# Order rules for VectorE's score tiles in a kernel with an order planned at build time

## The chip, the cores and the metric

One core of one Trainium2 chip. The metric is the device time of one execution in microseconds, the median of several runs. An execution has five engines with a queue of instructions each: TensorE (matmuls), VectorE, ScalarE, GpSimd and SyncE (which issues most DMAs).

## The reference

Two independent parts of 2048 tokens and width 640 are computed and laid side by side in the output of 1280 columns.

```python
# part A: a diagonal state-space layer, a recurrence over the tokens
Bu = einsum("bld,pd->blp", x, B_bar)
h = Lam_bar * h + Bu[:, t]                        # complex, for each t
y = 2 * einsum("blp,dp->bld", hs, C).real + x * Dskip
# part B: attention with 32 heads of width 20 that share one key and one value
q = (x @ wq).reshape(B, S, 32, 20); k = x @ wk; v = x @ wv
p = softmax(q @ k.T * 20 ** -0.5)
out = (p @ v).reshape(B, S, 640) @ wo
```

## The kernel before

**Tiles.** The scores of part B are cut into 2048 tiles of 128 keys x 512 queries of one head. A *block* is a group of four heads for 512 queries: 64 tiles, 16 of each head; there are 32 blocks. Part A, the projections and the output products run as tasks beside them.

**Two ways to the exponential.** A tile's scores are made by one matmul of 32 rows (`score`). Then either ScalarE computes exp of two or three tiles at once from PSUM into a ring `PR` of 24 columns (L1378), or VectorE reads the tile from PSUM into an integer buffer of `BIG` (`fill_d`, L1569; the page shows it as L811), an approximate exponential in the bits of a bf16. VectorE's way needs four versions of the tile (`SHIFTS`): the first read and three copies with a number added, made by VectorE (L811, BIG<-BIG) or GpSimd (L1673). Each version takes a buffer of its own until it has been used; `d_free` lists the free ones. A tile of ScalarE costs one matmul with V (PV, MB<-PR,VP), a tile of VectorE four (MB<-BIG,VS). PV matmuls of the four heads of a block run as a quad, side by side in four column groups.

**PSUM.** There are two *slots* of three banks each (SC) and two single banks (MB): one for the sums of PV, one for tasks. A fill (`fill`) writes a slot with three score matmuls. If the third bank is given to VectorE (`own`), ScalarE's exp covers two tiles; otherwise it covers three. A slot can be filled again when both its exp and VectorE's read of its third bank are done. VectorE may also get tiles in a free task bank (`extra`, `d_source`).

**The order.** Every instruction is a step with an assumed duration; at build time a list scheduler (`Schedule`) plays the engines forward, takes at each moment the ready step of the best priority, and so writes down one fixed order for each engine. Twelve such orders are made, eleven of them with small random shifts of the tasks' due times, and the one with the earliest planned end is built. Waits are semaphores placed from that order. So a rule changed in the choice of tiles changes the order of all engines from there on.

**Choice of VectorE's tiles.** `want_own` and `want_d` limit their share (`SHARE` 0.29 of all tiles so far) and ask for free buffers. `take_d` takes the tile from the block that `d_block` names: the current one, `act_block`, while more than `AHEAD` = 10 of its tiles remain, else the next. Of the block's four heads it takes the one with the fewest tiles given to VectorE (`d_turn`). `can_d` refuses a tile of a block that PV has not come to yet (`b > self.pv_b`) unless as many buffers are free as a tile needs plus all copies still due for the block in hand (`due_copies`).

**What waits for what.** An exp waits for its fill and for its columns of `PR` to have been read by PV (`h.prev` in `fill`). PV of a block starts after that of the block before has been read out (L1740).

Of the kernel before, what the change touches and what calls it, by code (L numbers as in the profile page):

```python
# [43 lines left out]
class Schedule:  # L44
# [13 lines left out]
    EARLIER = {"dve": 40.0, "act": 8.0}  # L58
# [371 lines left out]
class Build:  # L430
# [477 lines left out]
    def constants(self):  # L908
# [14 lines left out]
        def select(t, pattern, op, v, base, mult, dur):  # L923
            return "pool", lambda e: e.affine_select(out=t, in_=t, pattern=pattern, compare_op=op, fill=v, base=base,
                                                     channel_multiplier=mult), dur
        adds = next(x for x in library_config.all_libraries if bass_isa.InstInt64Add in x.instructions)
        self.adds_op = self.pool(lambda e: e.load_library(adds), 100, prio=0.1)
        many("ident", [fill(p.ident[:], 0.0, 110),
                       select(p.ident[:], [[-1, 128]], ALU.not_equal, 1.0, 0, 1, 300)])
        one = bass.AP(tensor=p.one, offset=0, ap=[[1, 128], [0, 256]])  # L930
        many("iota", [fill(p.one[:], 1.0, 80),
                      ("dve", lambda e: e.tensor_tensor_scan(p.iota[:], one, one, -1.0, ALU.mult, ALU.add), 670)])
        self.c_op["wkz"] = self.dve(lambda e: e.memset(p.wkr[:], 0.0), 110, writes=["wkr"], prio=0.2)
        many("tload", [fill(p.tload[:], 0.0, 80)])
        many("VP", [fill(p.VP[:], 0.0, 280), fill(p.VP[:, :, 20:21], 1.0, 100)])
        many("VZ", [fill(p.VZ[:], 0.0, 80)])
# [405 lines left out]
    def fill(self, op, i):  # L1342
        p = self
        t, banks = self.slots[i]
        n = min(self.cap[i], NTILE - self.tile_n)
        extra, used, own = [], set(), None
        if n == 3 and self.want_own():
            own = self.take_d(used)
        if own is not None:
            n = 2  # L1350
        while len(extra) < 4 - self.cap[i] and self.want_d(len(extra), own is not None):
            m = self.take_d(used)
            if m is None:
                break
            extra.append(m)
        tiles = [self.take_tile(used) for _ in range(n)]
        h = self.pr_take(n)
        keys = [f"PR{h.index + x}" for x in range(n)]
        ents = []
        for x, m in enumerate(tiles):  # L1360
            b, kc, j = self.score(op, m, t[:, 512 * x:512 * x + 512], banks[x])
            ents.append((b, kc, j, p.PR[:, h.index + x, :]))
        first = [] if own is None else [self.fill_d(op, own, banks[2])]
        if first:
            other = self.slot_last[1 - i][0]
            begin = self.s.t + self.mmt(512, 4) + 200
            if other.eng == "act":
                begin = max(begin, other.start + other.dur if other.start is not None else self.s.t + other.dur)
            first[0].due = begin + 2 * (0.8333 * 1024 + 64) - self.REFILL
        for m in extra:  # L1370
            self.fill_d(op, m)
        n_mm = len(op.fns)
        self.board(op, used)
        op.reads = sorted(set(op.reads))
        op.dur = self.mmt(512, n_mm + (len(op.fns) > n_mm))
        op.load = 128.0 * n_mm
        dst = p.PR[:, h.index:h.index + n, :]
        ex = self.act(lambda e: e.activation(dst, t[:, 0:512 * n], ACT.Exp, scale=1.0 / UNIT),  # L1378
                      0.8333 * 512 * n + 64, table="exp",
                      deps=[op], reads=[b.key for b in banks[:n]], writes=keys, prio=0.5,  # L1380
                      gate=lambda: all(x.taken and x.left == 0 and self.s.done(x.users) for x in h.prev))

        def on_start(_):
            h.taken, h.left, h.prev = True, n, []
            self.waiting.remove(h)
        self.waiting.append(h)
        ex.hook = on_start
        self.slot_last[i] = [ex] + first
        for (b, kc, j, rhs), key in zip(ents, keys):
            self.pvq[b][j].append((p.VP[:, kc, 0:32], kc, rhs, key, ex, h, "VP"))  # L1390
            self.pv_filled[b] += 1
# [35 lines left out]
    def want_own(self):  # L1427
# [4 lines left out]
        self.firsts = [o for o in self.firsts if o.start is None]  # L1432
        return len(self.d_free()) > len(self.SHIFTS) - 1

    firsts = []
    LAG = 120

# [42 lines left out]
        self.tile_n += 1  # L1480
        return 64 * b + 4 * self.rem[b][j].popleft() + j

    AHEAD = 10

    def d_block(self):

        b = self.act_block()
        return b if self.remaining(b) > self.AHEAD else b + 1

    def take_d(self, used):  # L1490

# [9 lines left out]
    def can_d(self):  # L1501
        b = self.d_block()
        if b >= NQB * NGG or not self.block_ready(b):
            return False
        if not self.block_seen(b):
            return False
        if b > self.pv_b and len(self.d_free()) < len(self.SHIFTS) + self.due_copies():
            return False
        return bool(self.rem[b][self.d_turn(b)])

# [948 lines left out]
```

## Time and profile before

| | us |
|---|---|
| median of 3 runs | 716.0 (715.95 to 716.43) |
| span of the profiled execution, first to last instruction | 714.5 |
| ScalarE busy | 695.0 |
| TensorE busy | 694.9 |
| VectorE busy | 627.5 |
| GpSimd busy | 429.3 |
| first exp starts | 21.17 |
| last exp ends | 704.76 |

The page gives no time of the profiled execution beside its span; the runs' times lie some 1.5 us above it. The granted TensorE clock is 1.000 over the span. TensorE's busy time is modelled at its ends: a matmul of 512 columns shows 0.38 us, while such matmuls follow each other some 0.22 us apart. In the rows below PEld are TensorE's weight loads, which carry its waits; "MB<-PR,VP" names what is written and what is read. A program's line L674 or L811 is a helper's, so the tiles tell the steps apart.

### The profile page before, as it was taken

The page shows a single profiled execution, that of the slowest core. Times are in us where ns is not written, and L with a number is a line of the kernel's source. Part 1 is how long each engine was busy: PE and PEld are TensorE (multiplying, and loading weights), DVE is VectorE, ACT ScalarE, POOL GpSimd, SP SyncE. Part 2 cuts the span into 40 slices and gives each one's busy share as a digit, 9 for nine tenths or more (in the row PEclk, how much of TensorE's full clock was granted, in tenths as well). Part 3 has the DMA queues.
Part 4 walks back from the last instruction along what each step waited for, and adds up shares of the span by engine and source line. Part 5 has one row for each costly group of instructions (what it writes and reads, how often), then busy time and mean ns, then how long its engine had stood idle before and what let it go on. Part 6 is the DMA issues. An engine that isn't in the chain of part 4 may idle for free.

```text
span 714.5 us, 26759 instructions
## 1 busy us (share of the span) xinstructions
PE 694.9 (97%) x11249; PEld 248.8 (35%) x11251; DVE 627.5 (88%) x1234; ACT 695.0 (97%) x699; POOL 429.3 (60%) x722
## 2 busy tenths in 40 slices
PE   8999999999999999999999999999999999999997
PEld 4322323344333443334433332334333333333323
DVE  6999989989998787879799999899999998876895
ACT  5999999999999999999999999999999999999995
POOL 2256672224785666866566657556568467688880
PEclk9999999999999999999999999999999999999999
DMA  9567831120110010112001010120000011110001
GB/s 230 138 172 175 166 87 38 37 49 17 40 48 11 19 27 24 40 31 52 20 18 28 19 34 20 42 56 20 9 17 20 12 25 36 34 23 21 26 8 39
DMA packets 77653, 34.44 MB, mean 48 GB/s; under 512 B 58414, under 2 KB 77534, under 8 KB 77534
## 3 DMA queue, kind: packets, MB, share of 16 engines
q1 hardware_dynamic: 75386, 31.68, 18.1%
q8 instruction: 90, 1.47, 0.9%
q10 hardware_dynamic: 2148, 1.05, 0.5%
q14 instruction: 29, 0.24, 0.1%
HBM read 11.53 MB, written 9.75 MB: 30 GB/s over the span
## 4 chain that ended last, share of the span: by engine, by line
PE 51%; ACT 44%; DVE 2%; DMA 1%; issue 0%; ACTq 0%
ACT PR L1378 44%; PE MB L674 19%; PE MB L744 14%; PE SC L674 12%; PE MB L754 5%; DVE BIG L811 1%; DMA vrow<-in_A_Lambda_im_dram 1%; PE SC L670 0%; ACT BIG L1046 0%; DVE pvsb L1740 0%; PE SC L1108 0%; ACT L1995 0%; ACTq L655 0%; DVE prod L806 0%; DVE BIG L1043 0%
## 5 line engine op out<-in xcount | busy, mean ns | idle before, releaser
L1378 ACT ACTIVATE PR<-SC 128x1024 bf16<-128x1024 f32 (+1 forms) x675 | 680.2, 1196 | 3.6 <-PE MB L674 2.1
L1673 POOL INT64_ADD BIG<-BIG x696 | 419.2, 618 | 251.5 <-DVE BIG L811 87.8
L811 DVE TENSOR_SCALAR BIG<-SC 128x512 int16<-128x512 f32 x516 | 345.1, 684 | 57.1 <-PE SC L674 51.1
L674 PE MATMUL SC<-QT,KT 32*128 32x512 bf16 x2003 | 263.8, 384 | 10.3 <-ACT PR L1378 5.2
L674 PE MATMUL MB<-BIG,VS 128*32 128x512 bf16 x2244 | 264.2, 384 | 0.2 <-DVE pvsb L1740 0.2
L674 PE MATMUL MB<-PR,VP 128*32 128x512 bf16 x1487 | 214.4, 384 | 0.2 <-DVE pvsb L1740 0.2
L674 PEld LDWEIGHTS SC<-QT,KT 32*128 32x128 bf16 x2003 | 67.6, 90 | 187.8 <-ACT PR L1378 122.2
L674 PEld LDWEIGHTS MB<-BIG,VS 128*32 128x32 bf16 x2244 | 63.1, 94 | 64.8 <-issue 41.2
L674 PEld LDWEIGHTS MB<-PR,VP 128*32 128x32 bf16 x1487 | 51.2, 94 | 47.1 <-issue 34.2
L811 DVE TENSOR_SCALAR BIG<-BIG 128x1024 int16<-128x1024 int16 (+1 forms) x154 | 56.6, 409 | 4.9 <-PE MB L674 4.0
L744 PE MATMUL MB<-CT,W 128*32 128x320 bf16 (+2 forms) x1004 | 54.1, 301 | 0.1
L744 PE MATMUL MB<-CA,W 128*32 128x512 bf16 (+1 forms) x640 | 35.1, 302 | 0.0
L744 PE MATMUL MB<-xaT,BA 128*32 128x256 bf16 x800 | 32.6, 275 | 0.0
L754 PE MATMUL MB<-xaT,BT 32*128 32x256 bf16 x160 | 30.9, 272 | 1.4 <-ACT PR L1378 1.3
L754 PE MATMUL MB<-diagD,xaT 32*128 32x128 bf16 x320 | 31.4, 217 | 0.0
L811 DVE TENSOR_SCALAR BIG<-MB 128x512 int16<-128x512 f32 x45 | 30.5, 678 | 0.5 <-PE MB L674 0.4
L744 PEld LDWEIGHTS MB<-CT,W 128*32 128x32 bf16 x1004 | 22.9, 96 | 15.0 <-issue 6.6
L754 PEld LDWEIGHTS MB<-diagD,xaT 32*128 32x128 bf16 x320 | 17.7, 92 | 29.9 <-ACT PR L1378 20.9
L1927 DVE CAST stg<-MB 128x512 bf16<-128x512 f32 x35 | 23.9, 683 | 2.7 <-PE MB L744 2.4
L806 DVE TENSOR_TENSOR prod<-MB,tab 128x1024 bf16<-128x1024 f32 x20 | 24.2, 1212 | 2.3 <-PE SC L674 1.6
L744 PE MATMUL MB<-xaT,BT 128*32 128x256 bf16 x640 | 25.9, 274 | 0.0
L744 PE MATMUL MB<-BIG 128*32 128x512 bf16 x320 | 24.8, 384 | 0.2
(162 smaller groups left out, 461.9 us busy)
## 6 DMA issues: line engine op xcount, KB each, us to landing
out_dram<-stg SPq DMA_DIRECT2D x31, 128.0 KB, 1.9
qd<-BIG SPq DMA_DIRECT2D x20, 128.0 KB, 1.8
QT<-qd SPq DMA_DIRECT2D x28, 80.0 KB
OP<-pvsb SPq DMA_DIRECT2D x105, 20.0 KB
rdP<-recs SPq DMA_DIRECT2D x105, 20.0 KB
lbd<-BA SPq DMA_DIRECT2D x5, 320.0 KB, 2.8
BA<-in_A_B_re_dram SPq DMA_DIRECT2D x1, 800.0 KB, 8.3
BA<-in_A_B_im_dram SPq DMA_DIRECT2D x1, 800.0 KB, 11.5
```

The costliest lines, as they stand in the source:

```text
L674: return lambda e: e.matmul(out, lhsT=lhsT, rhs=rhs, start=start, stop=stop, **kw)
L744: x = e.matmul(out[32 * j:32 * j + 32], lhsT=lhsT[:, 32 * j:32 * j + 32], rhs=rhs, start=start, stop=r.end is tag, tile_position=(0, 32 * ...
L754: return lambda e: e.matmul(out, lhsT=lhsT[at], rhs=rhs[at], start=False, stop=r.end is tag, tile_position=(32 * row, 0), skip_group_check ...
L806: return lambda e: e.tensor_tensor(out, a, b, op)
L811: return lambda e: e.tensor_scalar(out, a, s1, s2, op0=op0, op1=op1)
L1378: ex = self.act(lambda e: e.activation(dst, t[:, 0:512 * n], ACT.Exp, scale=1.0 / UNIT), 0.8333 * 512 * n + 64, table="exp", deps=[op], re ...
L1673: op.fns.append(lambda e: e.int64_add(words(dst), words(src), add))
L1927: ev = self.dve(lambda e: e.tensor_copy(st, bank.ap), 645, deps=[prev], reads=[bank.key], writes=[key], prio=self.EV, gate=(lambda: last.e ...
```

## The change

Three rules in the choice of VectorE's tiles are changed; no instruction is of a new kind.

1. `in_time`: a third bank is given to VectorE only if the planner expects VectorE to have read it by the time that the exp of the same slot ends, with 100 ns to spare. Otherwise the exp takes three tiles.
2. `d_block`: VectorE goes over to the next block's tiles when 14 of the current block's tiles remain (`AHEAD + EARLIER`), but stays, down to 3 remaining (`AHEAD - LATER`), as long as the number of tiles that it has had of this block is not a multiple of four.
3. `can_d`: for a block that PV has not come to, 4 free buffers (`ROOM`) and as many as there are due copies, but at most 2 of these (`CAP`), are enough.

```diff
@@ fill
-        if n == 3 and self.want_own():
+        if n == 3 and self.want_own() and self.in_time(i):
             own = self.take_d(used)
@@ new
+    def in_time(self, i):
+        s = self.s
+        other = self.slot_last[1 - i][0]
+        begin = s.t + self.mmt(512, 4) + 200
+        if other.eng == "act":
+            begin = max(begin, other.start + other.dur if other.start is not None else s.t + other.dur)
+        at = max(s.free["dve"], s.t + self.mmt(512, 4) + 200)
+        for o in self.firsts:
+            if o.start is None:
+                at = max(at, s.seen(o.deps[0], "dve")) + 605
+        return at + 605 + 110 <= begin + 2 * 512 * 0.8333 + 64 + self.SPARE
+
+    SPARE = 100
@@ d_block
-    AHEAD = 10
+    EARLIER, LATER = 4, 7
+    AHEAD, CAP, ROOM = 10, 2, 4
 
         b = self.act_block()
-        return b if self.remaining(b) > self.AHEAD else b + 1
+        left = self.remaining(b)
+        if left > self.AHEAD + self.EARLIER:
+            return b
+        if left > self.AHEAD - self.LATER and sum(self.d_per[b, j] for j in range(4)) % 4:
+            return b
+        return b + 1
@@ can_d
-        if b > self.pv_b and len(self.d_free()) < len(self.SHIFTS) + self.due_copies():
+        if b > self.pv_b and len(self.d_free()) < self.ROOM + min(self.due_copies(), self.CAP):
             return False
```

## The prediction, made before the changed kernel ran

> **What bounds the kernel now.** I read the page's busy line first, then the chain, the groups kept apart by shape, the waits, and last the timelines of ScalarE and TensorE.
>
> ```profile
> PE 694.9 (97%) x11249; PEld 248.8 (35%) x11251; DVE 627.5 (88%) x1234; ACT 695.0 (97%) x699; POOL 429.3 (60%) x722
> PE 51%; ACT 44%; DVE 2%; DMA 1%; issue 0%; ACTq 0%
> L1378 ACT ACTIVATE PR<-SC 128x1024 bf16<-128x1024 f32 x538 | 504.2, 1104 | 3.0 <-PE MB L674 1.8 <-PE SC L674 0.7
> L1378 ACT ACTIVATE PR<-SC 128x1536 bf16<-128x1536 f32 x137 | 192.0, 1555 | 0.6 <-PE MB L674 0.3
> L811 DVE TENSOR_SCALAR BIG<-SC 128x512 int16<-128x512 f32 x516 | 345.1, 684 | 57.1 <-PE SC L674 51.1 <-PE MB L674 1.8 <-POOL BIG L1673 0.2
> L811 DVE TENSOR_SCALAR BIG<-MB 128x512 int16<-128x512 f32 x45 | 30.5, 678 | 0.5 <-PE MB L674 0.4
> PEld SC L674 <- ACT PR L1378: 122.2, 292, 0.9
> PEld SC L674 <- DVE BIG L811: 41.2, 96, 0.9
> ```
>
> ScalarE runs 675 exps and stands still only 3.6 us ahead of them; TensorE waits 122.2 us for it before score fills and 41.2 us for VectorE's reads of third banks. So ScalarE sets the pace from its first exp to its last, and TensorE matters where a fill or a probability-times-V matmul (PV) comes so late that an exp has to wait.
>
> ```profile
> 21.17 13.86 ACT L1378 ACTIVATE PR<-SC 128x1024 bf16<-128x1024 f32 x15 [0.21 <-PE SC L674]
> 678.26 26.50 ACT L1378 ACTIVATE PR<-SC 128x1024 bf16<-128x1024 f32 x26 [0.99 <-PE MB L674]
> 706.34 0.38 ACT L1745 ACTIVATE pvsb<-MB 128x256 bf16<-128x256 f32 x1 [1.58 <-PE MB L674]
> ```
>
> The first exp ends at 22.19, so the other 14 of the first row end (13.86 - 1.02) / 14 = 0.917 us apart. In the second row 26.50 - 1.02 holds 19 more exps of two tiles and 6 of three (by the program's order): (25.48 - 17.42) / 6 = 1.344 us each. All exps at these pitches would end at 22.19 + 537 x 0.917 + 137 x 1.344 = 698.75; the last ends at 704.76. **The waits inside cost 6.0 us**, and nothing else is to be won in the long middle.
>
> Going through the ends of single exps, 28 come over 0.03 us late. 11 of them, 3.59 us, wait for a PV that stands on TensorE behind their own fill and frees the PR columns they write. 8 (1.08 us) follow a fill, or a ride ahead of it, held by VectorE's reads; 2 (0.71 us, exps 406 and 550) have too much TensorE work ahead of their fill; 7 (0.91 us) are small and mixed; the rest rounds to -0.28. This is a case of the first kind:
>
> ```profile
> 346.52 0.39 PE L674 MATMUL SC<-QT,KT 32*128 32x512 bf16 x3
> 346.84 0.61 PE L674 MATMUL MB<-BIG,VS 128*32 128x512 bf16 x8
> 347.28 0.39 PE L674 MATMUL MB<-PR,VP 128*32 128x512 bf16 x4
> 347.60 0.10 PEld L674 LDWEIGHTS SC<-QT,KT 32*128 32x128 bf16 x3 [0.42 <-ACT PR L1378]
> 347.72 2.86 ACT L1378 ACTIVATE PR<-SC 128x1024 bf16<-128x1024 f32 x3 [0.47 <-PE MB L674]
> ```
>
> The fill starts at 346.52 and three quads (four matmuls side by side) of PV follow, 0.32 us later and then 0.22 apart; only after the third may the exp write. It loses 0.58 us.
>
> **The change, part by part**
>
> *Counts.* The built order has 556 VectorE tiles for 561 (518 third banks for 516, 38 lent banks for 45), so ScalarE gets 1492 tiles for 1487: 540 exps of two tiles, again 137 of three, and one of a single tile at the end. The order up to the 26th exp is unchanged on ScalarE, so the start stays.
>
> *ScalarE's sum.* To the end of the third exp from the last, which releases the last fill: before, two exps of three tiles follow (2.69 us); after, one of three and the single one. All exps grow by 2 x 0.917 plus the single one; what follows the release shrinks by 1.344 minus the single one. The single one cancels: 1.83 + 1.34 = **+3.18 us** up to the last fill. No row shows it; between 0.43 (three tiles less two) and 0.60 (L1922, one tile alone) it ends at most 1.94 after the release, before PV does, so both ends give the same.
> [...]
>
> *The end.* After the last fill, before has 14 full quads of PV and then three singles of one head, which share a column group and so go one after another: 17 steps. After has 9 full quads and 3 of three heads: 12 steps. A step is 0.217 us (702.45 to 705.92 for 16 of them), so **-1.08 us**. The single exp lies inside. VectorE has 10 copies for 13 behind its last score read, so it stays ahead (before, it was done with them at 703.2). The output steps are the same. Without a change in the waits: +2.10 us.
>
> *PV behind its fill.* This is where "next heads' tiles with a few free buffers" and "equal counts" act: they set what PV has ready. In the trace one quad behind the fill costs 0.11 to 0.29 us after an exp of two tiles (six cases, mean 0.18), nothing after one of three; three quads 0.58, or 0.16 and 0.20 after one of three; four quads after one of three 0.45; and one case, 678.26, took 1.10, where the next fill stood ahead of that PV and waited for VectorE. In the new order: four of one quad after two tiles (0.72), two of three quads after three tiles (0.36), three of four quads after three tiles (1.36), the others covered, none with a fill in between. Sum 2.44 for 3.59: **-1.15**; bounds 1.9 and 3.2.
>
> *Too much TensorE work.* Stretches beside a two-tile exp that hold 4.5 quads or more: 13 for 23. 0.71 x 13/23 = 0.40: **-0.31** (bounds 0 and -0.71). The sum of TensorE's work is the same: 20 VS and 5 VP matmuls are -15, 24 KT,VZ fillers are added (6.6 us / 104 each, 1.5 us), and fillers run only where nothing else is ready.
>
> *Third banks in time.* No instruction goes: 137 exps of three tiles stay. Between two third-bank reads VectorE's work, by its rows' durations, exceeds the exps' time by over 0.8 us at 34 places for 45. 1.08 x 34/45 = 0.82: **-0.27** (bounds +0.3 and -1.08). VectorE itself loses 5 reads (0.67 each by 345.1/516), 4 copies of 1024 and 7 of 512, some 6.6 us; hidden, since VectorE is 2% of the chain. GpSimd's 696 adds stay 696. DMAs are as many, in near the same order.
>
> Sum: 3.18 - 1.08 - 1.15 - 0.31 - 0.27 = **+0.37 us** on the span of 714.5, or 714.9. The runs' median is 716.0, 1.5 us around the span, which the change doesn't touch: **716.4 us**. About 0.2% (1.4 us) is what a measurement of this kernel can tell from no change, and +0.37 lies inside.
>
> **Rivals**
>
> *PV runs behind on the chip (slower).* Tiles of the next heads hold four buffers each until PV comes to them. Taken with four free buffers and at most two due copies counted, they can leave VectorE and GpSimd without room to write copies of the heads in hand; their PV come late, and PR columns are freed late. For it: eight exps of the new order wait for two quads or more, or for a ride and a quad, behind their fill (60, 317, 407, 417, 593, 606, 610, 633) where six did, and TensorE already waits 9.5 us for GpSimd's copies. Against it: the three longest all stand after an exp of three tiles, which covers most of them. One more stall of the 1.10 us size makes it +1.47 and decides; with half of another one 718.0 us.
>
> *The third banks win (faster).* If the rule removes the late reads altogether, and the small mixed waits with them, since most follow a late fill: -1.08 - 0.91 in place of -0.27, PV at its low price of 1.9 (-1.69): 3.18 - 1.08 - 1.69 - 0.31 - 1.99 = -1.89, or 714.1 us. Against it: VectorE's idle time is 57 us already and third banks grow by two, so the rule moved them rather than thinned them.
>
> *The change does not do what it says.* As many third banks, as many three-tile exps; the waits come up elsewhere at the same 6.0 us. Then five more tiles on ScalarE are all that is left: +2.10, 718.1 us, slower.
>
> **How the numbers follow.** The counts of the order speak for the forecast in three of four terms, but they are counts, and one long stall weighs as much as its whole gain: 0.55. PV behind on the chip: 0.22. Nothing but a shuffle: 0.10. Third banks win: 0.13. The forecast's own range is 715.0 to 717.4 (PV 1.9 to 3.2, VectorE -1.08 to +0.3). To hold 8 in 10 it reaches up to both slower cases, 718.4, and down to 714.7, leaving out most of the faster one. Faster 0.13, same 0.55, slower 0.32.
>
> **What would show it.** Right: 540 and 137 exps at pitches of 0.917 and 1.344; waits inside of 4.0 to 4.7 us; PV after the last fill 2.6 us long; exps 317, 407 and 610 late by 0.4 us each; TensorE's wait for VectorE's reads below 41.2 us. Wrong: waits inside of 5.3 us or more (slower), of 2.5 or less (faster), a stall near 1 us at a change of heads, idle time of TensorE before PV that GpSimd ends well above 9.5 us, or PV after the last fill as long as before.

## The result, and the profile after

The changed kernel takes 717.82 us (median of 18 runs, 716.88 to 721.42) against 716.30 for the kernel before, run beside it. The ratio is 1.0024, with a 95% interval of 1.0018 to 1.0030. So it is slower by 1.5 us, a little more than a measurement of this kernel can tell from no change. The profiled execution has a span of 715.7 us for 714.5.

The page of the changed kernel, its line of busy times and its chain:

```profile
PE 690.7 (97%) x11260; PEld 247.5 (35%) x11260; DVE 623.8 (87%) x1218; ACT 696.6 (97%) x702; POOL 431.5 (60%) x722
ACT 63%; PE 32%; DVE 3%; DMA 1%; issue 1%; ACTq 0%
```

Its groups, kept apart by shape:

```profile
L1378 ACT ACTIVATE PR<-SC 128x1024 bf16<-128x1024 f32 x540 | 510.0, 1120 | 3.7 <-PE SC L674 2.2 <-PE MB L674 1.0
L1378 ACT ACTIVATE PR<-SC 128x1536 bf16<-128x1536 f32 x137 | 196.8, 1589 | 0.2
L1378 ACT ACTIVATE PR<-SC 128x512 bf16<-128x512 f32 x1 | 0.8, 764 | 0.0
```

Its waits:

```profile
PEld SC L674 <- ACT PR L1378: 116.4, 277, 0.8
PEld SC L674 <- DVE BIG L811: 42.9, 97, 0.9
PEld MB L674 <- POOL BIG L1693: 5.7, 25, 0.2
```

And two rows of its timeline of ScalarE, the first exps and the read-out of the last PV:

```profile
20.86 20.27 ACT L1378 ACTIVATE PR<-SC 128x1024 bf16<-128x1024 f32 x22 [0.21 <-PE SC L674]
...
707.62 0.39 ACT L1765 ACTIVATE pvsb<-MB 128x256 bf16<-128x256 f32 x1 [1.35 <-PE MB L674]
```

The exps are as counted: 540, 137 and one single. The idle time of weight loads put down to VectorE's reads has not fallen; that put down to GpSimd's copies has, to 5.7 us. Before, the row was:

```profile
PEld MB L674 <- POOL BIG L1673: 9.5, 42, 0.2
```

Whether such rows are waits at all is asked below, at the PR ring. A new thing stands in the first group: more of ScalarE's idle time is put down to fills (SC, 2.2 us) than to PV (MB, 1.0); before it was 0.7 and 1.8.

An execution can be cut into four pieces that add up to its span: the end of the first exp, the exps' own time from there at 0.917, 1.344 and 0.49 us (the last for the single one, by its end), the waits inside, and what follows the last exp. For the kernels below this gives, in us:

| kernel | first exp ends | exps' own | waits inside | of these, PV behind its fill | after last exp | span |
|---|---|---|---|---|---|---|
| before | 22.19 | 676.56 | 6.01 | 3.59 | 9.69 | 714.5 |
| changed | 21.88 | 678.88 | 5.50 | 2.43 | 9.46 | 715.7 |
| changed, code shifted by 72 | 21.96 | 678.88 | 4.18 | 2.48 | 9.46 | 714.5 |
| before, PR ring without waits | 22.85 | 676.56 | 4.94 | 0 | 9.69 | 714.0 |
| changed, shifted by 72, PR ring without waits | 22.21 | 678.88 | 3.22 | 0 | 9.45 | 713.8 |
| rule 1 alone, shifted by 72 | 22.06 | 680.53 | 5.40 | 1.21 | 9.33 | 717.3 |
| rule 2 alone, shifted by 168 | 22.01 | 680.04 | 4.96 | 1.55 | 8.75 | 715.8 |
| rule 3 alone | 21.98 | 676.19 | 12.53 | 4.36 | 9.05 | 719.7 |
| `LATER` = 3, shifted by 90 | 21.83 | 676.92 | 2.73 | 0.85 | 9.26 | 710.7 |

The first column moves by up to a microsecond, and by 0.66 us between two kernels of the same order (22.19 and 22.85), so single profiles are compared from the second column on. Before and changed: +2.32 - 0.51 - 0.23 = +1.58 us, and the runs' medians say +1.52.

Going through the late exps one by one, as before: nine of the changed kernel wait for a PV behind their fill (2.43 us), eight follow a fill held by VectorE's reads (1.18), three small ones follow other late fills (0.25), the rest rounds to -0.30. That is 3.56 of the 5.50. The other 1.94 us are two exps, numbers 308 and 461 (exps are numbered from 0), that no list of mine had:

```profile
341.25 2.02 ACT L1378 ACTIVATE PR<-SC 128x1024 bf16<-128x1024 f32 x2 [0.65 <-PE SC L674]
...
493.21 1.94 ACT L1378 ACTIVATE PR<-SC 128x1024 bf16<-128x1024 f32 x2 [1.08 <-PE SC L674]
```

Both wait for a fill. In the changed kernel's timeline of TensorE's weight loads, this is what stands ahead of these fills:

```profile
339.27 0.10 PEld L744 LDWEIGHTS MB<-CA,W 128*32 128x32 bf16 x2
340.22 0.10 PEld L744 LDWEIGHTS MB<-CA,W 128*32 128x32 bf16 x2 [0.85 <-issue]
...
491.04 0.10 PEld L744 LDWEIGHTS MB<-CA,W 128*32 128x32 bf16 x1
492.38 0.10 PEld L744 LDWEIGHTS MB<-CA,W 128*32 128x32 bf16 x3 [1.24 <-issue]
```

TensorE stands still in the middle of a group of four equal loads, and for "issue": it waits for nothing that the profile shows. The next load is instruction 10,689 of TensorE in the first case and 15,809 in the second. Both numbers are 193 more than a multiple of 256, and they are 20 x 256 apart. (The count goes by the trace's records; a second trace of the same kernel, below, has two fewer.) The page's queue line says what comes in such units:

```profile
q8 instruction: 90, 1.47, 0.9%
```

1.47 MB in 90 pieces is 16.3 KB each, and TensorE has 23,106 instructions, 90 times 256 and 66 more. The first fetch of this queue starts when TensorE has begun 202 of them and the last when it has begun 23,015, a mean of 256.3 from one to the next. So its program looks to be fetched in blocks of 256. Fetches on this queue start at 337.83 and 490.10, last 1.1 and 0.9 us, and TensorE goes on 1.28 and 1.34 us after their ends. Both blocks ahead of the pauses are mostly matmuls of 128 columns, and TensorE does each block in 2.8 us; the shortest block of the kernel before lasts 3.1 us, and no such pause is in it.

Theory A, then: the forecast's waits came out about right in sum, and what it lacked is two pauses of TensorE that hang on where the new order's dense stretches fall in its code. The rival: the two late fills belong to the new order itself, by what is queued there or by late data. A second question is whether the PR ring, on which the forecast's largest gain in waits stood, is where the gain came from.

### The profile page after: what moved, and what is told of

Read it like the earlier page. It is cut to its first block, busy times and chain, and to the rows that moved or that the text cites. A ratio compares the mean times of both kernels' runs of the same rounds, so it can differ in the third digit from the quotient of the medians.

```text
span 715.7 us, 26740 instructions
## 1 busy us (share of the span) xinstructions
PE 690.7 (97%) x11260; PEld 247.5 (35%) x11260; DVE 623.8 (87%) x1218; ACT 696.6 (97%) x702; POOL 431.5 (60%) x722
## 3 DMA queue, kind: packets, MB, share of 16 engines
q8 instruction: 90, 1.47, 0.9%
## 4 chain that ended last, share of the span: by engine, by line
ACT 63%; PE 32%; DVE 3%; DMA 1%; issue 1%; ACTq 0%
ACT PR L1378 62%; PE MB L674 11%; PE MB L744 9%; PE SC L674 7%; PE MB L754 4%; DVE BIG L811 2%; DMA BIG<-in_B_wq_dram 1%; PE SC L670 0%; DVE prod L806 0%; PE SC L1108 0%; DVE stg L1947 0%; DVE pvsb L1760 0%; DVE OP L806 0%; ACT PR L1942 0%; DVE iota L932 0%
## 5 line engine op out<-in xcount | busy, mean ns | idle before, releaser
L1693 POOL INT64_ADD BIG<-BIG x696 | 421.5, 620 | 253.2 <-DVE BIG L811 122.2
L811 DVE TENSOR_SCALAR BIG<-SC 128x512 int16<-128x512 f32 x518 | 349.7, 686 | 65.3 <-PE SC L674 57.4
L674 PE MATMUL MB<-BIG,VS 128*32 128x512 bf16 x2224 | 255.6, 384 | 0.6 <-DVE pvsb L1760 0.4
L674 PEld LDWEIGHTS MB<-BIG,VS 128*32 128x32 bf16 x2224 | 61.5, 94 | 64.7 <-issue 42.6
L674 PEld LDWEIGHTS MB<-PR,VP 128*32 128x32 bf16 x1492 | 52.8, 94 | 49.2 <-issue 36.5
L811 DVE TENSOR_SCALAR BIG<-BIG 128x1024 int16<-128x1024 int16 (+1 forms) x143 | 54.3, 416 | 4.3 <-PE MB L674 3.1
L744 PE MATMUL MB<-xaT,BA 128*32 128x256 bf16 x800 | 31.1, 275 | 0.1
L754 PE MATMUL MB<-xaT,BT 32*128 32x256 bf16 x152 | 29.4, 272 | 1.3 <-ACT PR L1378 1.2
L811 DVE TENSOR_SCALAR BIG<-MB 128x512 int16<-128x512 f32 x38 | 25.7, 677 | 0.2 <-PE MB L674 0.2
```

Source lines behind the costliest of these rows:

```text
L674: return lambda e: e.matmul(out, lhsT=lhsT, rhs=rhs, start=start, stop=stop, **kw)
L744: x = e.matmul(out[32 * j:32 * j + 32], lhsT=lhsT[:, 32 * j:32 * j + 32], rhs=rhs, start=start, stop=r.end is tag, tile_position=(0, 32 * ...
L754: return lambda e: e.matmul(out, lhsT=lhsT[at], rhs=rhs[at], start=False, stop=r.end is tag, tile_position=(32 * row, 0), skip_group_check ...
L811: return lambda e: e.tensor_scalar(out, a, s1, s2, op0=op0, op1=op1)
L1693: op.fns.append(lambda e: e.int64_add(words(dst), words(src), add))
```

## Experiments

**Moving the code.** Some of the warm-up matmuls at the start are cut into four of 128 columns. They do the same work, and all that follows stands at another place modulo 256. Each extra matmul is two instructions, so 12 of them shift the code by 12 x 3 x 2 = 72.

```diff
     def warm_last(self, op):
         self.pvbank.last = [op]
+        p, n = self, 128
+        self.warm_n += 1
+        if self.warm_n <= 12:
+            op.fns = [p.mm(p.pvbank.cols(n * i, n * i + n), p.PR[:, 0, 0:128], p.PR[:, 0, n * i:n * i + n], True, True)
+                      for i in range(4)]
+
+    warm_n = 0
```

> The changed order, with TensorE's instructions shifted by 72: twelve of the warm-up matmuls at the start (512 columns) are cut into four of 128 columns. Every later instruction of every engine is the same. Theory A (code blocks): in the profile of the changed kernel TensorE pauses at 339.27 (0.95 us) and 491.05 (1.33 us) without a wait, both at instruction 193 of 256 by its own count, the place where one 16 KB block of code ends; the block before had lasted 2.83 and 2.86 us. Shifted by 72, the shortest block of the same stream lasts 3.35 us, so no such pause is left, the two exps (308 and 461) lose their 0.76 and 1.19 us, and the time falls by about 1.9 us from 717.8 to 715.9, that is 0.4 us below the kernel before. Theory B (the pauses belong to the new order: to its matmuls, its reads or its DMAs at that place): they stay at the same matmuls, 717.8 us.

Measured: 716.63 us (715.93 to 719.79) where before reads 716.81; ratio 0.9999 (0.9981 to 1.0017). In its timeline of ScalarE the first of the two places is one row of eleven exps without the standstill, and in that of the weight loads one shorter pause is left near the second:

```profile
334.93 10.57 ACT L1385 ACTIVATE PR<-SC 128x1024 bf16<-128x1024 f32 x11
```

```profile
490.27 0.10 PEld L744 LDWEIGHTS MB<-CT,W 128*32 128x32 bf16 x4 [0.48 <-issue]
```

The nine waits for PV are the same to 0.06 us, and the waits inside fall from 5.50 to 4.18 us. That is 1.3 us and not the 1.9 forecast: behind the shorter pause exp 460 is late by 0.41 us, and in the row of eleven exp 310 is late by 0.25, where exp 308 had been late by 0.76.

The same edit with 7 matmuls shifts by 42; the densest stretch then lies across other ends of blocks.

```diff
-        if self.warm_n <= 12:
+        if self.warm_n <= 7:
```

> The same with seven warm-up matmuls cut into four, a shift of 42. Theory A: three blocks of code now last only 2.57 us (about 488), 2.77 us (238) and 2.84 us (336), so three pauses where there were two, the one at 488 the longest; 718.5 to 719.5 us. Theory B: 717.8 us, pauses at the same matmuls as in the changed kernel.

Measured: 719.8 us (717.25 to 723.08), ratio 1.0029 (1.0005 to 1.0053). Its weight loads show two long pauses, both 191 over a multiple of 256, and so at other places of the order than in the changed kernel:

```profile
111.53 0.09 PEld L674 LDWEIGHTS SC<-QT,KT 32*128 32x128 bf16 x1 [1.16 <-issue]
...
346.36 0.10 PEld L744 LDWEIGHTS MB<-CT,W 128*32 128x32 bf16 x3 [2.02 <-issue]
```

One exp of 0.97 and one of 1.93 us of wait follow from them. The forecast of the places was right for the one at 346 alone: the shortest block, named as the one with the longest pause, has none, the one near 238 has 0.40 us (at 246.45), and the pause at 111 was not among the three. This profile also has some 4 us of waits at exps 6 to 12. ScalarE stands still 2.35 us ahead of exp 6, for a release that its row does not name, TensorE with it, and from 31.8 to 35.2 us the granted clock is 0.5; exps 10 to 12 lose 1.39 us there and just behind. What began it stays open, so the 10.66 us inside are not compared with the others.

The kernel before can be given the pauses that it doesn't have: 9 warm-up matmuls cut into eight shift it by 126.

```diff
-        p, n = self, 128
+        p, n = self, 64
...
-        if self.warm_n <= 12:
+        if self.warm_n <= 9:
...
-                      for i in range(4)]
+                      for i in range(8)]
```

> The kernel before, with nine warm-up matmuls cut into eight, a shift of 126 instructions. Unshifted, its shortest block of code lasts 3.12 us and it shows no pause. Shifted, the block that begins near 234 lasts 2.24 us, the next shortest 3.07. Theory A: one pause of 1.2 to 1.6 us near 236 and some 1.2 us more, 717.5 us. Theory B: no pause, 716.3 us.

Measured: 719.11 us (718.45 to 721.11), ratio 1.0030 (1.0014 to 1.0046). Two pauses have come, both 190 over a multiple of 256, and the waits inside are 8.50 us for 6.01:

```profile
237.34 0.10 PEld L674 LDWEIGHTS SC<-QT,KT 32*128 32x128 bf16 x2 [0.59 <-issue]
...
632.59 0.09 PEld L674 LDWEIGHTS MB<-BIG,VS 128*32 128x32 bf16 x1 [0.83 <-issue]
```

A pause in a stretch where TensorE is late anyway delays several exps (208, 211 and 212 around the first, 601 and 603 around the second), and smaller waits at 312, 460 and 461 are new too. The kernel lost 2.3 us by the medians where 1.2 had been forecast, and the second pause had not been named. With this, the core of theory A holds: the same order is slower or not by where its code lies, and the order before pays as well. It is not the smaller warm-up matmuls that do it, since the same kind of edit made the changed kernel faster at 72 and slower at 42. Which blocks end in a pause, and how long it is, the theory did not foretell.

Last, the changed kernel once more, in a later session:

> The changed kernel itself, beside the others on the same chip: 717.8 where before reads 716.4 to 716.8, with two pauses of TensorE of about 1 us at 339 and 491 us again, at the same places of its code (193 modulo 256 instructions).

Measured: 718.56 us (717.43 to 725.2) where before reads 716.94, ratio 1.0028 (1.0008 to 1.0048). The two pauses are there again, at instructions 10,687 and 15,807 (191 over a multiple of 256):

```profile
341.33 0.10 PEld L744 LDWEIGHTS MB<-CA,W 128*32 128x32 bf16 x2 [1.15 <-issue]
...
493.49 0.10 PEld L744 LDWEIGHTS MB<-CA,W 128*32 128x32 bf16 x3 [1.24 <-issue]
```

**The PR ring without waits.** A PV matmul of a ScalarE tile still waits for the tile's exp, but reads 512 columns of KT, which are never written again. So no exp has to wait for PV.

```diff
@@ pv
             lhs, kc, rhs, key, _, h, vk = e
+            rhs = p.KT[:, 0:512] if vk == "VP" else rhs
...
+            if vk == "VP":
+                op.after.append(e[4])
+                key = "KT0"
             op.reads += [f"{vk}{kc // 4}", vk, key]
```

> Before's order unchanged, but a PV matmul of a ScalarE tile reads 512 columns of KT in place of the tile's PR columns (it still waits for the tile's exp), so no exp ever waits for a PV to free PR columns; the output is thereby not the attention's. By the prediction's sum the PV-behind-its-fill waits (3.59 us in before) go and nothing takes their place: 3.6 us below before, 712.8 where before reads 716.4, with waits inside of 2.4 us. Rival, the waits move to the next limit (VectorE's reads, late fills): under 2 us below before.

Measured: 715.74 us (714.84 to 723.5) where before reads 716.93; ratio 1.0003 (0.9980 to 1.0025), so the runs alone show no gain. In the profiles the exps' waits fall by 1.07 us. The 3.59 us of PV behind its fill are gone, but 2.5 us have come up elsewhere: the exp two places on, in the same slot, is late instead. Exp 398 waited 0.45 us in before and not at all here, while exps 400 and 402, on time before, now wait 0.24 and 0.12. Exp 649's 1.10 us is gone, and 651 waits 0.66. The reason is to be seen in the fills of this stretch. In TensorE's timeline of the kernel before:

```profile
428.94 0.39 PE L674 MATMUL SC<-QT,KT 32*128 32x512 bf16 x3
429.26 0.83 PE L674 MATMUL MB<-BIG,VS 128*32 128x512 bf16 x12
429.92 0.39 PE L674 MATMUL MB<-PR,VP 128*32 128x512 bf16 x4
430.23 0.10 PEld L674 LDWEIGHTS SC<-QT,KT 32*128 32x128 bf16 x3 [0.42 <-ACT PR L1378]
430.24 0.39 PE L674 MATMUL SC<-QT,KT 32*128 32x512 bf16 x3
...
431.54 0.39 PE L674 MATMUL SC<-QT,KT 32*128 32x512 bf16 x3
```

And in that of the kernel with the free ring:

```profile
429.02 0.39 PE L674 MATMUL SC<-QT,KT 32*128 32x512 bf16 x3
...
430.33 0.39 PE L674 MATMUL SC<-QT,KT 32*128 32x512 bf16 x3
...
431.63 0.39 PE L674 MATMUL SC<-QT,KT 32*128 32x512 bf16 x3
```

The fills come 1.30 us apart in both (1.31 once). The rows of the first 1.30 us show why: a fill, 0.32 us on three quads, 0.22 apart, then a fourth, and 0.32 us behind it the next fill. TensorE has that much to do between them and doesn't care whether an exp waited. In this stretch the wait for PV was real, but it stood in the place of a wait for the next fill.

The weight load of the fill at 430.23 says something about the prediction too. It has 0.42 us of idle time put down to ScalarE, and yet the matmuls around it follow each other without a gap. It is one of the 292 loads whose 122.2 us the prediction read as TensorE waiting for ScalarE; their mean is 0.42. Loads of a fill that wait for nothing show nearly as much (0.36 each), and what the fills' matmuls themselves stood still for ScalarE is far less. In the kernel before:

```profile
PEld SC L674 <- issue: 18.1, 50, 0.7
PE SC L674 <- ACT PR L1378: 5.2, 18, 0.5
```

With the free ring, the load at 431.62 has the same 0.42 us, now for "issue". So most of that idle time is no wait, and TensorE had far less room than the prediction's reading gave it.

> The same substitution in the changed kernel with 12 warm-up matmuls cut into four (TensorE's code shifted by 72 instructions, so that no code pause of a microsecond is in it). By the prediction's sum 2.44 us of waits go, and what is left between this and before_free is +3.18 - 1.08 - 0.31 - 0.27 = +1.5 us: about 714.3. If the PR ring is not where the change wins, the two free kernels differ by as little as the two whole ones without code pauses did (-0.1 to +0.3 us).

Measured: 715.93 us (715.17 to 720.36), ratio 0.9997 (0.9984 to 1.0010), 0.2 us above the other free kernel and not 1.5. Its waits fall by 0.96 us for the 2.48 taken away, and what the changed kernel has less in waits than before is 4.94 - 3.22 = 1.72 us without the ring's waits and 6.01 - 4.18 = 1.83 with them. So, by these four profiles, the gain in waits is not the ring's: it is there with and without the ring's waits.

**Each rule alone.** Rule 3 alone is the changed kernel without the first two edits:

```diff
-        if n == 3 and self.want_own() and self.in_time(i):
+        if n == 3 and self.want_own():
...
-        left = self.remaining(b)
...
-        return b + 1
+        return b if self.remaining(b) > self.AHEAD else b + 1
```

> The third rule alone (next block's tiles with 4 free buffers and at most 2 due copies; third banks and change of block as before). Its order has 562 VectorE tiles (561 before), 542 exps of two tiles and 134 of three; up to the last fill ScalarE's sum and the PV steps behind it are together 1.24 us shorter than before. By the prices of the prediction its PV behind fills cost 0.45 us more (two of them with the next fill in between, as at 678 before). Steps of the prediction: -0.8 us, 715.5 us. The rival that copies come late because next heads' tiles hold the buffers: PV pays more, 717 us or above, and TensorE's idle time ended by GpSimd's copies rises above 9.5 us.

Measured: 720.65 us (719.18 to 727.41), ratio 1.0053 (1.0026 to 1.0079), a miss by 5 us. ScalarE has less to do than before (676.19 us), and waits 12.53 us: 4.36 for PV (3.67 counted), 2.36 behind VectorE's reads, 5.98 behind other late fills, of which 1.76 are two pauses at 191 over a multiple of 256 and 1.24 an exp at the start. What I had counted from the order covers a third of it. The rival's time came, but not its sign: the idle time of TensorE's loads put down to GpSimd's copies is 8.4 us, below the 9.5 of before.

Rule 1 alone, with the code shifted by 72:

```diff
-        left = self.remaining(b)
...
-        return b + 1
+        return b if self.remaining(b) > self.AHEAD else b + 1
...
-        if b > self.pv_b and len(self.d_free()) < self.ROOM + min(self.due_copies(), self.CAP):
+        if b > self.pv_b and len(self.d_free()) < len(self.SHIFTS) + self.due_copies():
```

> The in_time rule alone (third banks to VectorE only if read in time), TensorE's code shifted by 72. Counted from its order: 535 exps of two tiles and 142 of three, so ScalarE's sum with the tail is +3.3 us against before; PV behind fills priced 1.12 for 3.22 us, -2.1. By the prediction's steps +1.2 us (717.6), or down to +0.1 (716.5) if all late third banks (1.08) go with it. Rival, the waits come up elsewhere at the same size: +3.3, 719.7.

Measured: 718.94 us (718.52 to 721.61), ratio 1.0036 (1.0023 to 1.0048). Waits for PV are 1.21 us (1.12 counted), so 2.4 us of them are gone, and those behind VectorE's reads, which this rule is about, fall to 0.77 for 1.08. But other late fills come to 3.70 us for 1.62; 0.55 of that is a code pause and 0.59 one exp (318), whose fill stands behind a step that waits for another result of VectorE. Against before it is +2.0 us by the medians and +2.6 by the ratio, between the forecast's +1.2 and the rival's +3.3.

Rule 2 alone, shifted by 168:

```diff
-        if n == 3 and self.want_own() and self.in_time(i):
+        if n == 3 and self.want_own():
...
-        if b > self.pv_b and len(self.d_free()) < self.ROOM + min(self.due_copies(), self.CAP):
+        if b > self.pv_b and len(self.d_free()) < len(self.SHIFTS) + self.due_copies():
```

> The d_block rule alone (equal counts for a group's four heads, and when VectorE turns to the next heads), TensorE's code shifted by 168 (12 warm-up matmuls cut into eight). Counted from its order: 531 exps of two tiles, 144 of three and one of one; ScalarE's sum with a tail of 7 steps +2.2 us against before; PV behind fills priced 1.28 for 3.22 us, -1.9. By the prediction's steps +0.2 us (716.6). Rival, the waits come up elsewhere: +2.2, 718.6. With code blocks whose matmuls take little over 2 us, two or three pauses of 0.5 to 1 us on top would be the code's.

Measured: 718.05 us (717.34 to 720.74), ratio 1.0022 (1.0011 to 1.0032). Waits for PV 1.55 us (1.28 counted), waits inside 4.96, 0.78 of them a code pause. Between the two theories; the counted gain of 1.9 us gave 1.0. All three rules alone are slower than before, each with 0.55 us or more of code pauses in its waits, and none is a part of the result that could be added to the others: each draws another order.

**Half of PV.** To take TensorE's load away, PV matmuls after the first of each head and block are done on 256 columns.

```diff
@@ pv
+            n = 512 if first else 256
-            op.fns.append(self.mm(bank.tensor[32 * j:32 * j + 32, bank.off:bank.off + 512], lhs, rhs,
+            op.fns.append(self.mm(bank.tensor[32 * j:32 * j + 32, bank.off:bank.off + n], lhs, rhs[:, 0:n],
```

> Before's order unchanged, but every PV matmul after the first of its head and block is done on 256 of its 512 columns, so half of the PV is left out and TensorE has some 100 us less to do. If the late exps (PV behind its fill, too much TensorE work) are all TensorE running full, as before_free suggests (taking the PR ring away won 1.1 us where 3.6 had been counted), most of before's 6.0 us of waits inside go and about 1.4 us, those of VectorE's reads, stay: 4.6 us below before plus 1.8 us of a shorter tail. If VectorE's reads set the late fills, the waits stay above 4 us.

> The same half PV in the changed kernel, TensorE's code shifted by 72. If what the change wins in waits (1.8 us in the traces) is TensorE's lateness, nothing of that is left to win here: this kernel is slower than before_half by ScalarE's +3.18 us less 5 steps of tail at half length (0.5), about +2.7 us, less what the third banks in time win (0.3). Rival, the win is VectorE's reads: about +0.9.

Measured: 717.33 us (714.93 to 723.94), ratio 1.0012 (0.9986 to 1.0038), and 719.09 us (715.54 to 725.12), ratio 1.0020 (0.9989 to 1.0050), where before reads 716.94. As times both are misses and decide nothing between the theories, because the granted clock changed: its mean lies between 0.972 and 0.988 in the runs of the one and between 0.964 and 0.988 in those of the other, where before has 0.992 to 1.000. A table of stretches of the half kernel made from before (us, busy time of PE, PEld, DVE, ACT and POOL, granted clock, DMA share, GB/s):

```profile
360.00:378.00 18.00, 14.82 (x240) 5.41 (x236) 17.17 (x34) 18.00 (x20) 10.37 (x18) 1.00 0.11 28
378.00:389.00 11.00, 10.04 (x174) 4.13 (x174) 9.03 (x15) 10.11 (x12) 8.45 (x15) 0.84 0.09 23
...
524.00:533.00 9.00, 8.74 (x152) 3.52 (x144) 6.97 (x12) 7.31 (x9) 6.13 (x11) 0.73 0.07 17
```

At full clock, 360 to 378, ScalarE is busy all the time. The 0.84 and 0.73 of the other two stretches are means: the clock granted is 0.50 from 378.6 to 382.0 and from 522.0 to 528.8 us, and 1.00 around that. There ScalarE loses 0.89 and 1.69 us. In the half kernel made from the changed one, it is 0.50 from 69.3 to 79.5 us. The late exps can still be sorted by the clock. In the half kernel made from before, 4.1 us of them start in such a stretch or within 2 us behind it, and 2.1 us elsewhere (0.92 of it exp 649), where before has 6.3 us in all; in the other half kernel it is 7.2 and 0.6 us. So at full clock most of the late exps are gone with TensorE's work, while VectorE's work is the same; this rests on one profile of each. Why the clock falls where TensorE's work was cut is not shown; the three stretches at 0.50 given here last 3.4, 6.8 and 10.2 us.

**A version that beats both.** From the orders of other constants I took the one that was best by three counts at once: ScalarE's own time, PV behind fills, and the work in the shortest block of code.

```diff
-    EARLIER, LATER = 4, 7
+    EARLIER, LATER = 4, 3
@@ warm_last
+        p, n = self, 128
+        self.warm_n += 1
+        if self.warm_n <= 15:
+            op.fns = [p.mm(p.pvbank.cols(n * i, n * i + n), p.PR[:, 0, 0:128], p.PR[:, 0, n * i:n * i + n], True, True)
+                      for i in range(4)]
```

> The changed kernel with LATER = 3 for 7 (VectorE stays longer with its block for equal counts) and TensorE's code shifted by 90 (15 warm-up matmuls cut into four), where every block of 256 instructions lasts as long as can be. Counted from its order: 534 exps of two tiles, 140 of three, 560 VectorE tiles; ScalarE's sum with a tail of 13 steps is -0.6 us against before, PV behind fills priced 0.85 for 3.22 us. If waits inside fall to the 4.2 us of the changed kernel without code pauses, it is 2.4 us below before, 714.2. Rival, waits grow as ScalarE's sum shrinks, because the sum of both is set by TensorE: about before's time.

Measured: 712.92 us (712.68 to 713.75) where before reads 716.94; ratio 0.9937 (0.9917 to 0.9957), and 1.3 us under the forecast. How long the fills' matmuls stand still for ScalarE:

```profile
PE SC L674 <- ACT PR L1385: 8.9, 28, 0.6
```

That is 8.9 us for 5.2 in before and 7.4 in the changed kernel, so TensorE is early somewhat more often. No pause for "issue" holds an exp. Waits inside are 2.73 us: 0.85 for PV (0.85 counted), 1.02 behind VectorE's reads, 1.09 behind other late fills, and -0.23 of rounding. Against before, by the table of pieces: +0.36 - 3.28 - 0.43 = -3.35 us, and -0.36 from the start. The rival, that waits grow as ScalarE's sum shrinks, is wrong here, though it fits rule 3 alone. Why this order has so few waits is not shown.

## Why the prediction was right or wrong

The time of 717.8 us lies inside the range of 714.7 to 718.4, and that is in part luck: the sum said 716.4, and the upper end of the range had been drawn out to cover slower cases of another kind. The forecast's own range is added up wrongly at its upper end, too: 3.2 for PV and +0.3 for the third banks give 716.4 + 1.33 = 717.7, not 717.4.

- **ScalarE's sum and the end: right.** Forecast +3.18 - 1.08 = +2.10 us. Exps' own time is +2.32 and what follows the last exp -0.23, in sum +2.09. PV after the last fill runs from 704.80 to the read-out at 707.62, 2.82 us; in before it was 702.45 to 706.34, 3.89: -1.07.
- **PV behind its fill: right as a count, wrong as a price.** 2.44 us forecast, 2.43 measured; exps 317, 407 and 610 lose 0.40, 0.46 and 0.48. But booking all of a wait as time to be won was wrong: taking 3.59 us of such waits out of before won 1.07 (30%), and 2.48 out of the changed kernel 0.96 (39%). By the difference of the two, the -1.15 of this term is worth some 0.1 us.
- **TensorE's room: misread.** Idle time of weight loads was read as TensorE waiting: 122.2 us for ScalarE, 41.2 for VectorE's reads, 9.5 for GpSimd's copies. It is 0.42, 0.43 and 0.23 us for each load, as much as loads show around which no matmul is held up. With so little room on TensorE, a wait taken from one exp came back at another.
- **Too much TensorE work, and the small mixed waits: right in direction, far too small.** 1.62 us in before, 1.31 forecast, 0.25 measured outside the two pauses (with the code shifted, 0.9 with what is left of the pauses). What of the three rules spread TensorE's work better stays open.
- **Third banks in time: wrong.** Forecast -0.27; measured 1.18 us for 1.08, and the loads' idle time put down to VectorE's reads is 42.9 us for 41.2. VectorE's own busy time fell by 3.7 us and not by 6.6, which stayed hidden either way. The count of 34 places for 45 did not price it. Rule 1 alone did lower these waits, to 0.77 us; in the order that all three rules draw nothing of that is left.
- **What was missing: TensorE's pauses, which hang on the place of its code.** The sentence "the sum of TensorE's work is the same" took it that the same work takes the same time. Two pauses of 0.95 and 1.33 us, from load to load, put 1.94 us on two exps. With the code shifted, where half a microsecond's pause is left, the changed kernel's profile is level with before's (714.48 and 714.46 us) and its runs with before's (ratio 0.9999): the forecast's +0.37 us came out as about zero (+0.26 by the table without the start). This missing term alone took the result from "no difference" to slower. That the rest agrees so well is luck as well: the three terms of waits were to give -1.73 us, and the shifted kernel's waits are 1.83 below before's, but none of the three terms had its price right.
- **The rivals.** PV did not run behind on GpSimd's copies: the loads that name them are 25 for 42. The third banks won nothing. The shuffle at +2.10 us and equal waits is nearest in time (718.1 forecast, 717.8 measured), but not in kind: the order's own waits fell by about 1.8 us, and the code's pauses gave 1.3 of that back.

Of the signs named beforehand, the counts, the three late exps and a shorter end came, PV after the last fill with 2.8 us for 2.6. The waits inside of 5.50 us were above the 5.3 that I had named as the mark of a wrong forecast.

## What to carry to other kernels

Where one engine is the pace and another is nearly full beside it (here ScalarE busy for 695.0 and TensorE for 694.9 of 714.5 us), a wait counted at one exp is not time to be won (3.59 us of such waits taken out won 1.07): ask what the full engine does next, and whether the following fill would have been late by as much. How full TensorE was showed here in the distance between its quads (0.22 us), not in the idle time ahead of its weight loads (0.42 us, put down to ScalarE at 430.23 in before and to "issue" at 431.62 with the free ring). Before a change of order is judged by a microsecond, look for idle time of a dense engine that waits for nothing, and see whether it recurs at one place modulo the size of a block of code (here at 190 to 193 modulo 256 instructions); a shift of the code then tells the order from its placing. Neighbouring constants of a planner gave 716.6 us (`LATER` 7) and 712.9 us (`LATER` 3) with the code placed well in both, so one order measured says little about the rule that drew it.

## What the runs showed of the hardware that was not expected

- TensorE paused 0.5 to 2.0 us, waiting for nothing that the profile shows, at 190 to 193 instructions over a multiple of 256. Most blocks ahead of such a pause were run in 2.3 to 3.5 us. No length decides alone: one of 3.1 us in before had no pause behind it, and one of 6.1 us, at 110 us with the code shifted by 42, had one of 1.16. In the two pauses of the changed kernel's first profile TensorE went on 1.28 and 1.34 us after the end of a fetch on the instruction queue (338.94 and 491.03 us); both fetches had ended by the time that the pauses began. That the fetch is the cause is argued from these times and from the block's size; that the pause hangs on the place in the code is shown by the shifts. Idle rows of 0.45 to 0.64 us for "issue" stand at other places of a block as well, in before too (0.64 at 68.04), and those are not explained by it.
- Cutting TensorE's busy time from 695 to 627 us made the kernel no faster than the noise (ratio 1.0012). The granted clock fell to 0.50 in several stretches of 3.4 to 10.2 us. Ahead of the one at 378.6 us, from 360 to 378 at a clock of 1.00, TensorE was busy for 14.82 of 18.00 us (82%); over the whole span it was 88%.
